# A fused attention and feed-forward kernel: inverse row sums of the first four jobs multiplied onto the result instead of onto the exponentials, and the low bits of all second-weight parts prepared on ScalarE

## The chip, the cores and the metric

The kernel runs on one core of one Trainium2 chip. The metric is device time in microseconds (us) of one execution. Three executions of the kernel before gave 1086.21, 1086.63 and 1086.92 us; the median is 1086.63.

## What is computed

Causal attention for 8 batches, 8 heads, 576 positions and a head width of 64, with a bias made of running sums of `s`, and after it a feed-forward layer with a piecewise quadratic activation:

```python
scores = scale * q @ k.T + min(bias, 0)            # bias[t, u] = -(cum[t] - cum[u]), cum = cumsum(max(s, 0))
attn = exp(where(causal, -1e9, scores) - rowmax)
attn = attn / (sum(attn, -1) + 1e-9)
x = (attn @ v)                                     # reordered to 4608 rows of 512
h = x @ w_in                                       # 512 -> 2048
g = where(h >= 1, h, where(h <= -1, 0, (h + 1) ** 2 / 4))
out = g @ w_out                                    # 2048 -> 512
```

The two weight matrices arrive as 64-bit numbers, 8 bytes an element.

## The kernel before

**Jobs.** The attention is cut into 64 jobs: for each batch, first the four head pairs with query rows 0 to 319 (tiles of 64, 128 and 128 rows), then the four pairs with rows 320 to 575 (two tiles of 128). A head of a tile goes through `scores`: TensorE makes the scores in PSUM (L439 in the first twelve jobs, L442 and L443 later), VectorE adds the mask, takes the row minimum and writes SBUF (L448), ScalarE turns it into exponentials with their row sums (L459).

**The first four jobs** (batch 0, first half) are "plain": all in 32-bit floats. When both heads of a tile have their exponentials, `plain_t` makes the inverse row sums `rs` on VectorE (L473, L474) and multiplies them onto the exponentials in place: GpSimd does the first head (L479), ScalarE the second (L477). Then TensorE transposes the scaled blocks into a PSUM bank `pp` (L482; two banks of the tag "h" take turns), and ScalarE copies them to `pt` (L483). One job later `att_out` multiplies `pt` with `v` (L531) into a bank `px` of the "y" tags. The four `px` stay in their banks until the scale of the first weights is known; then `x_split` makes two 16-bit parts of each for the feed-forward, on ScalarE (L559) and VectorE (L560). All later jobs go another way (`weights_t`, 16-bit parts, transposed by DMA).

**Weights.** Each matrix comes in 16 parts of 128 x 512 elements, called `wir` for the first and `wor` for the second. `decode` rebuilds a part: ScalarE takes the high word (L208), VectorE shifts it (L209), takes its peak (L211), and ORs in low bits (L223). These low bits are prepared before, either on ScalarE (L219, 8-bit source, bias and scale) or on VectorE (L222, a 16-bit shift by 13); the table `ACT_LOW` says which parts go to ScalarE: the even ones of both matrices. `split` then makes the two 16-bit parts that the matmuls use: L260 on ScalarE, and L268 on VectorE or L263, L265 and L266 on GpSimd and ScalarE. It needs a scale from the peaks of a group of parts. For the second matrix there are two groups of eight; for each, `scale` runs a small chain of VectorE and TensorE steps: a transpose of the peaks (`row_wo`), a maximum (`top_wo`), a broadcast by matmul (`col_wo`) through banks of the tags "y2" and "y3", and a reciprocal (`r_wo`, L237 and L238). The first matrix has one such chain for all of it (`row_wi`, `top_wi`, `t_wi` cast, `col_wi`, `t_wi` copy, `shares`); the first `x_split` waits for its end.

**The feed-forward.** For each half of a batch, 16 steps `ffn_h` (12 matmuls each, L601), an eviction on ScalarE and VectorE (`u` L613, L616, L617, then the parts of `g`, L627 on ScalarE and L628 on GpSimd), and 16 steps `ffn_y` (12 matmuls each, L640). The `u` tiles have four buffers of tag "u".

**Order.** The program text interleaves all this by slots: one part of the first weights every three attention slots, then the decode of the second weights beside the first feed-forward steps. A scheduler then orders each engine's queue; what an engine has in its queue runs in that order.

Of the kernel before, what the change touches and what calls it, by code (L numbers as in the profile page):

```python
# [9 lines left out]
F32 = mybir.dt.float32  # L10
# [4 lines left out]
AF = mybir.ActivationFunctionType  # L15
ALU = mybir.AluOpType
# [4 lines left out]
B, H, S, D = 8, 8, 576, 64  # L21
DM, DFF = 512, 2048
P = 128
# [7 lines left out]
QT = [(0, 64, 64)] + [(64 + P * i, P, 64 + P * (i + 1)) for i in range(4)]  # L31
HALF = [(0, 320, (0, 1, 2)), (320, 256, (3, 4))]
BIG = 1e9
EPS = 1e-9
# [18 lines left out]

Y_LAG = 2

ACT_LOW = {'wi': range(0, 16, 2), 'wo': range(0, 16, 2)}
POOL_LO = {'wi': (0, 2, 4, 6, 8, 10), 'wo': range(1, 16, 2)}
POOL_SCALE = ('wi',)

# [17 lines left out]
def attention_ffn(ctx: ExitStack, tc: tile.TileContext, qT, kT, vn, s, w_in, w_out, yT):  # L77
    nc = tc.nc
    LOADQ, CUMQ, FIRSTQ = nc.sync, nc.scalar, nc.sync
    V, A, G, T = nc.vector, nc.scalar, nc.gpsimd, nc.tensor  # L80

    cp = ctx.enter_context(tc.tile_pool(name="cp", bufs=1))
    ap = ctx.enter_context(tc.tile_pool(name="ap", bufs=2))
    gp = ctx.enter_context(tc.tile_pool(name="gp", bufs=2))
    dp = ctx.enter_context(tc.tile_pool(name="dp", bufs=1, space=DRAM))
    ps_s = ctx.enter_context(tc.tile_pool(name="ps_s", bufs=2, space=PSUM))
    ps_h = ctx.enter_context(tc.tile_pool(name="ps_h", bufs=2, space=PSUM))
# [10 lines left out]
    ident = cp.tile([P, P], F32, name="ident")  # L98
# [78 lines left out]
    class Weights:  # L177
        def __init__(self, name, src, held, out, tag, groups, by_rows=False):
# [8 lines left out]
            self.raw = {}  # L187
            self.act_low, self.pool_lo = ACT_LOW[name], POOL_LO[name]

# [151 lines left out]
    X = {}  # L341

    NP = B * NPAIR
    raws, pts_, vts, pbs, sums = {}, {}, {}, {}, {}

    def whole(n, hf):
        return jobs.index((n, hf)) < F32_JOBS

    def plain(n, hf):
        return jobs.index((n, hf)) < PLAIN_JOBS  # L350

    def operands(n, hf):
        return whole_tiles[jobs.index((n, hf)) % 2]
# [70 lines left out]
    def scores(n, i, hd, c0, c1):  # L424

        off, R, W = QT[i]
        qo = off - HALF[i // 3][0]
        if hd == 0 and c0 == 0:
            sums[n, i] = ap.tile([P, 2], F32, tag="sm", bufs=4, name=f"sm{n}_{i}")
            pbs[n, i] = []  # L430
        if c0 == 0:
            Pt = ap.tile([P, SP], F32, tag="p", bufs=4, name=f"p{n}_{i}_{hd}")
            pbs[n, i].append(Pt)
            G.memset(Pt[:R, W:W + D], 0.0)
        Pt = pbs[n, i][hd]
        sc = ps_s.tile([P, 512], F32, tag="s", name=f"s{n}_{i}_{hd}_{c0}")
        if whole(n, i // 3):
            Q, K = operands(n, i // 3)
            T.matmul(sc[:R, :c1 - c0], Q[:KC, hd, qo:qo + R], K[:KC, hd, c0:c1], start=True, stop=True)  # L439
        else:  # L440
            (Q1, K1), (Q2, K2) = split_tiles
            T.matmul(sc[:R, :c1 - c0], Q1[:, hd, qo:qo + R], K1[:, hd, c0:c1], start=True, stop=False)  # L442
            T.matmul(sc[:R, :c1 - c0], Q2[:KC, hd, qo:qo + R], K2[:KC, hd, c0:c1], start=False, stop=True)  # L443
        mn = mins.pop((n, i, hd), None)
        m2 = ap.tile([P, 1], F32, tag="mn", bufs=6, name=f"mn{n}_{i}_{hd}_{c0}")
        mo = 448 - off + c0
        with tc.high_priority(offset=TTR_LEAD):
            ttr[0] = V.tensor_tensor_reduce(  # L448
                out=Pt[:R, c0:c1], in0=sc[:R, :c1 - c0], in1=mask[:R, mo:mo + c1 - c0],
                scale=-0.125, scalar=3.0e38 if mn is None else mn[:R],  # L450
                op0=ALU.add, op1=ALU.min, accum_out=m2[:R],
            ).ins
        if late:
            with tc.issue_after(ttr[0]):
                late.pop(0)()
        if c1 < W:
            mins[n, i, hd] = m2
            return
        A.activation(  # L459
            Pt[:R, :W], Pt[:R, :W], AF.Exp, bias=m2[:R], scale=-1.0, accum_out=sums[n, i][:R, hd:hd + 1]  # L460
        )
        if hd:
            weights_t(n, i)

    def plain_t(n, i):

        off, R, W = QT[i]
        h_off, N, tiles = HALF[i // 3]
        if i == tiles[0]:
            pts_[n, i // 3] = ap.tile([P, 2 * (tiles[-1] + 1), N], F32, tag="pt", bufs=2, name=f"pt{n}_{i // 3}")  # L470
        PT = pts_[n, i // 3]
        rs = ap.tile([P, 2], F32, tag="rs", bufs=4, name=f"rs{n}_{i}")
        V.tensor_scalar(rs[:R], sums.pop((n, i))[:R], EPS, 2.0 ** -12, ALU.add, ALU.mult)  # L473
        V.reciprocal(rs[:R], rs[:R])  # L474
        for hd, Pt in enumerate(pbs.pop((n, i))):
            if hd:
                A.activation(Pt[:R, :W], Pt[:R, :W], AF.Copy, scale=rs[:R, 1:])  # L477
            else:
                G.tensor_scalar(Pt[:R, :W], Pt[:R, :W], rs[:R, :1], 1.0, ALU.mult, ALU.mult)  # L479
            pp = ps_h.tile([P, 512], F32, tag="h", name=f"pp{n}_{i}_{hd}")  # L480
            for j in range(i + 1):
                T.transpose(pp[:, j * R:(j + 1) * R], Pt[:R, j * P:(j + 1) * P], ident[:R, :R])  # L482
            A.copy(  # L483
                PT[:, hd:2 * (i + 1):2, off - h_off:off - h_off + R],
                pp[:, :(i + 1) * R].rearrange("p (j r) -> p j r", r=R),
            )

    def weights_t(n, i):

        off, R, W = QT[i]  # L490
        hf = 0 if i < 3 else 1
        h_off, N, tiles = HALF[hf]
        if plain(n, hf):
            plain_t(n, i)
            return
        if i == tiles[0]:
            pts_[n, hf] = ap.tile([P, 4 * (tiles[-1] + 1), N], F16, tag="pt", bufs=2, name=f"pt{n}_{hf}")
        PT = pts_[n, hf]
        PB = ap.tile([P, i + 1, 4, P], F16, tag=f"pb{hf}", name=f"pb{n}_{i}")
        rs = ap.tile([P, 2], F32, tag="rs", bufs=4, name=f"rs{n}_{i}")  # L500
        V.tensor_scalar(rs[:R], sums.pop((n, i))[:R], EPS, 2.0 ** -12, ALU.add, ALU.mult)
        V.reciprocal(rs[:R], rs[:R])  # L502
        tiles2 = pbs.pop((n, i))
        pv, pw = (Pt[:R, :W + D].rearrange("p (j c) -> p j c", c=P) for Pt in tiles2)
        his, los = ([PB[:R, :, 2 * hd + l, :] for hd in range(2)] for l in range(2))
        G.tensor_scalar(his[0], pv, rs[:R, :1], 1.0, ALU.mult, ALU.mult)  # L506
        A.activation(tiles2[1][:R, :W], tiles2[1][:R, :W], AF.Copy, scale=rs[:R, 1:])  # L507
        G.tensor_scalar(his[1], pw, 1.0, 1.0, ALU.mult, ALU.mult)  # L508
        G.tensor_tensor(los[1], pw, his[1], ALU.subtract)  # L509

        def rest():
            V.scalar_tensor_tensor(los[0], pv, rs[:R, :1], his[0], ALU.mult, ALU.subtract)  # L512
            nc.sync.dma_start_transpose(
                out=PT[:, :4 * (i + 1), off - h_off:off - h_off + R],
                in_=PB[:R].rearrange("p j g c -> p (j g c)"),
            )

        late.append(rest)

    def att_out(n, hf):  # L520

        b, p = n // NPAIR, n % NPAIR
        h_off, N, tiles = HALF[hf]
        nj = tiles[-1] + 1
        PT = pts_.pop((n, hf))
        if plain(n, hf):
            px = ps_y.tile([P, 512], F32, tag=f"y{p}", name=f"px{n}_{hf}")
            for j in range(nj):
                lo = max(0, j * P - h_off)
                for hd in range(2):  # L530
                    T.matmul(  # L531
                        px[hd * D:(hd + 1) * D, lo:N], vraw[b, p][:, j, hd * D:(hd + 1) * D],
                        PT[:, 2 * j + hd, lo:], start=(j == 0), stop=(j == nj - 1),
                    )
            held[n, hf] = px
            return
        px = ps_s.tile([P, 512], F32, tag="s", name=f"px{n}_{hf}")
        steps = [(j, vl, pl) for j in range(nj) for vl, pl in ((0, 0), (1, 0), (0, 1))]
        for m, (j, vl, pl) in enumerate(steps):
            lo = max(0, j * P - h_off)  # L540
            for hd in range(2):
                T.matmul(  # L542
                    px[hd * D:(hd + 1) * D, lo:N],
                    vts[n][:, vl, j, hd * D:(hd + 1) * D],
                    PT[:, 4 * j + 2 * hd + pl, lo:],
                    start=(m == 0), stop=(m == len(steps) - 1),
                )
        x_split(n, hf, px, w1.shares)

    held = {}  # L550
# [162 lines left out]
    with tc.high_priority(offset=SCALE_LEAD):  # L713
# [4 lines left out]
        for c in range(NW - NKT, NW):  # L718
            w1.split(c)
    att_out(*jobs[NPAIR - 1])  # L720
    for n, hf in jobs[:NPAIR]:
        x_split(n, hf, held.pop((n, hf)), shares0)
# [61 lines left out]
```

## Time and profile before

| | |
|---|---|
| median of three runs | 1086.63 us |
| the profiled execution | 1084.4 us |
| its span | 1082.6 us |
| granted TensorE clock over the span | 0.992 |
| busy: TensorE, VectorE, ScalarE, GpSimd | 1010.8, 851.4, 722.7, 665.9 us |

The span begins with the first instruction and ends with the last; 1.8 us of the execution lie around it. Times in the rows count from the span's start. PE is TensorE, DVE VectorE, ACT ScalarE, POOL GpSimd, SP the queue that issues most transfers. The first weights are decoded from about 6 to 69 us, the plain jobs run from 14 to 92 us, the first `ffn_h` matmul starts at 94 us, and the second weights are decoded from 35 to 131 us.

### The profile page before, as it was taken

The numbers are of one execution on the slowest core, as the hardware profiler recorded it, in microseconds if no ns is written. First come the engines' busy times: TensorE is split into PE (matmuls) and PEld (weight loads), VectorE is DVE, ScalarE is ACT, GpSimd is POOL, SyncE is SP. The second block draws the span as 40 slices with busy tenths as digits, with TensorE's granted clock in tenths as the row PEclk, the third lists the DMA queues.
The fourth block names the chain that finished last, engine by engine and source line by source line (L and its number), as shares of the span: only waits on it lengthen the run. The fifth ranks groups of instructions, "written<-read, shape, count | busy, mean of one in ns | idle before, by whom it ended". The sixth has DMA issues, their size and how long they took to land.

```text
span 1082.6 us, 24990 instructions
## 1 busy us (share of the span) xinstructions
PE 1010.8 (93%) x8494; PEld 775.7 (72%) x8494; DVE 851.4 (79%) x2370; ACT 722.7 (67%) x1707; POOL 665.9 (62%) x1139
## 2 busy tenths in 40 slices
PE   2657799999999999999999999999999999999998
PEld 1334466787778777887778777787778777887787
DVE  6898975688788888887788787788788787887533
ACT  4886774667577755877577765777577755877433
POOL 3764775675567656665577656665567656665422
PEclk9999899999999999999999999999999999999999
DMA  8974444455376873777366553765376662666300
GB/s 257 226 210 143 102 96 102 89 134 143 78 169 146 137 139 83 171 140 141 91 164 142 141 132 93 162 135 143 80 171 142 135 142 68 158 127 137 70 25 20
DMA packets 300839, 140.33 MB, mean 130 GB/s; under 512 B 237608, under 2 KB 286632, under 8 KB 300712
## 3 DMA queue, kind: packets, MB, share of 16 engines
q1 hardware_dynamic: 291008, 128.80, 53.1%
q10 hardware_dynamic: 9704, 9.93, 3.0%
q8 instruction: 67, 1.10, 0.4%
q14 instruction: 60, 0.49, 0.1%
HBM read 71.00 MB, written 9.73 MB: 75 GB/s over the span
## 4 chain that ended last, share of the span: by engine, by line
PE 66%; DVE 14%; ACT 7%; DMA 5%; issue 4%; POOL 2%; ACTq 1%; SPq 1%; DVEq 0%; POOLq 0%
PE h L601 27%; PE y L640 27%; PE px L542 4%; PE s L442 3%; PE s L443 3%; DVE pb L512 2%; DVE p L448 2%; PE s L439 2%; DVE h L616 2%; ACT u L613 1%; ACT p L459 1%; DVE K2s L398 1%; DMA v<-in_v_dram 1%; DMA wir<-in_moe_w_in_dram 1%; ACT o L654 1%
## 5 line engine op out<-in xcount | busy, mean ns | idle before, releaser
L601 PE MATMUL h<-x,WI 128*128 128x256 f16 (+1 forms) x3072 | 456.9, 289 | 4.0 <-ACT x L559 2.7
L640 PE MATMUL y<-g,WO 128*128 128x256 f16 (+1 forms) x3072 | 447.6, 287 | 4.0 <-DVE WO L268 2.6
L601 PEld LDWEIGHTS <-WI 128*128 128x128 f16 x3072 | 286.8, 99 | 94.4 <-issue 12.7
L640 PEld LDWEIGHTS <-WO 128*128 128x128 f16 x3072 | 286.8, 98 | 87.4 <-issue 5.0
L628 POOL TENSOR_TENSOR g<-u,g 128x320 f16<-128x320 f32 (+1 forms) x256 | 206.8, 808 | 162.1 <-ACT g L627 154.2
L459 ACT ACTIVATE p<-p,mn 64x64 f32<-64x64 f32 (+4 forms) x320 | 179.6, 561 | 107.2 <-DVE mn L448 82.3
L613 ACT ACTIVATE u<-h,ub,us 128x320 f32<-128x320 f32 (+1 forms) x256 | 149.5, 585 | 130.9 <-PE h L601 126.7
L616 DVE SCALAR_TENSOR_TENSOR h<-h,ws,u 128x320 f32<-128x320 f32 (+1 forms) x256 | 132.8, 519 | 89.1 <-ACT u L613 85.6
L506 POOL TENSOR_SCALAR pb<-p,rs 128x256 f16<-128x256 f32 (+4 forms) x148 | 93.4, 631 | 138.3 <-DVE rs L502 85.7
L509 POOL TENSOR_TENSOR pb<-p,pb 128x256 f16<-128x256 f32 (+4 forms) x148 | 156.6, 1058 | 9.8
L448 DVE CUSTOM_DVE_ANT_0 p<-s,mask 64x64 f32<-64x64 f32 (+4 forms) x320 | 135.0, 422 | 31.4 <-PE s L443 20.4
L512 DVE SCALAR_TENSOR_TENSOR pb<-p,rs,pb 128x256 f16<-128x256 f32 (+4 forms) x148 | 127.1, 859 | 21.3 <-POOL pb L506 20.8
L617 DVE SCALAR_TENSOR_TENSOR u<-u,r,h 128x320 f32<-128x320 f32 (+1 forms) x256 | 130.5, 510 | 7.3
L442 PE MATMUL s<-K1s,Q1s 128*128 128x288 f32 (+4 forms) x312 | 118.1, 379 | 9.8 <-DVE Q1s L397 4.1
L507 ACT ACTIVATE p<-p,rs 128x192 f32<-128x192 f32 (+4 forms) x148 | 84.3, 569 | 49.6 <-DVE rs L502 47.1
L627 ACT CAST g<-u 128x320 f16<-128x320 f32 (+1 forms) x256 | 108.2, 423 | 11.0 <-DVE u L617 10.8
L508 POOL TENSOR_SCALAR pb<-p 128x256 f16<-128x256 f32 (+4 forms) x148 | 89.1, 602 | 19.6 <-ACT p L507 14.6
L443 PE MATMUL s<-K2s,Q2s 68*128 68x288 f32 (+4 forms) x312 | 96.1, 308 | 0.0
L542 PEld LDWEIGHTS <-vt 128*64 128x64 f16 x1464 | 67.3, 111 | 19.7 <-issue 14.6
L542 PE MATMUL px<-pt,vt 128*64 128x256 f16 (+3 forms) x1464 | 77.9, 254 | 1.3 <-DMA pt<-pb 1.0
L442 PEld LDWEIGHTS s<-K1s,Q1s 128*128 128x128 f32 (+1 forms) x312 | 56.6, 181 | 19.1 <-PE s L443 4.0
L398 DVE TENSOR_TENSOR K2s<-rk,K1s 64x1152 fp32r<-64x1152 f32 (+1 forms) x52 | 63.2, 1216 | 5.9 <-ACT K1s L395 4.7
(130 smaller groups left out, 1035.0 us busy)
## 6 DMA issues: line engine op xcount, KB each, us to landing
rk<-in_k_dram SPq DMA_DIRECT2D x56, 288.0 KB
wir<-in_moe_w_in_dram SPq DMA_DIRECT2D x16, 512.0 KB
v<-in_v_dram SPq DMA_DIRECT2D x32, 256.0 KB
wor<-in_moe_w_out_dram SPq DMA_DIRECT2D x16, 512.0 KB
rk<-in_k_dram SPq DMA_DIRECT2D x48, 160.0 KB
rq<-in_q_dram SPq DMA_DIRECT2D x48, 160.0 KB
rq<-in_q_dram SPq DMA_DIRECT2D x56, 128.0 KB
out_dram<-o ACTq DMA_DIRECT2D x32, 160.0 KB
```

The lines of the kernel that those rows point to most:

```text
L442: T.matmul(sc[:R, :c1 - c0], Q1[:, hd, qo:qo + R], K1[:, hd, c0:c1], start=True, stop=False)
L448: ttr[0] = V.tensor_tensor_reduce(out=Pt[:R, c0:c1], in0=sc[:R, :c1 - c0], in1=mask[:R, mo:mo + c1 - c0], scale=-0.125, scalar=3.0e38 if m ...
L459: A.activation(Pt[:R, :W], Pt[:R, :W], AF.Exp, bias=m2[:R], scale=-1.0, accum_out=sums[n, i][:R, hd:hd + 1])
L509: G.tensor_tensor(los[1], pw, his[1], ALU.subtract)
L512: V.scalar_tensor_tensor(los[0], pv, rs[:R, :1], his[0], ALU.mult, ALU.subtract)
L542: T.matmul(px[hd * D:(hd + 1) * D, lo:N], vts[n][:, vl, j, hd * D:(hd + 1) * D], PT[:, 4 * j + 2 * hd + pl, lo:], start=(m == 0), stop=(m ...
L601: T.matmul(h[:, :N], WI[4 * kt + ft // 4][:, wl, ft % 4 * P:(ft % 4 + 1) * P], x[:, kt, xl], start=(n == 0), stop=(n == 3 * NKT - 1),)
L613: first = A.activation(u, h[:, :N], AF.Relu, bias=ubi[b], scale=usc[b]).ins
L616: V.scalar_tensor_tensor(h[:, :N], h[:, :N], wsc[b], u, ALU.mult, ALU.max)
L617: V.scalar_tensor_tensor(u, u, r, h[:, :N], ALU.min, ALU.mult)
L628: G.tensor_tensor(g[:, 1], u, g[:, 0], ALU.subtract)
L640: T.matmul(ys[b, hf, m][:, :N], WO[8 * (m // 2) + ft // 2][:, wl, c0:c0 + P], g[:, gl], start=(ft == 0 and n == 0), stop=(ft == NFT - 1 an ...
```

## The change

1. `ACT_LOW` for the second weights holds all 16 parts: the low bits of the eight odd ones are prepared by L219 on ScalarE instead of L222 on VectorE.
2. In the plain jobs the exponentials are transposed as they are, head by head, right after L459. The eight-line loop with the multiplications on GpSimd and ScalarE is gone. The inverse row sums are still made on VectorE, in tiles of an own tag with six buffers.
3. `att_out` of a plain job turns the inverse row sums into a row: six matmuls with a broadcast of `rp` as weights and the identity as moving data fill a bank `rx` of tag "h" (64 equal rows for each head). ScalarE copies `rx` to `z` in SBUF (tag "u"), VectorE multiplies it with `px` into `z`. `x_split` reads `z`; the `px` banks are free earlier.

```diff
-ACT_LOW = {'wi': range(0, 16, 2), 'wo': range(0, 16, 2)}
+ACT_LOW = {'wi': range(0, 16, 2), 'wo': range(16)}
...
-        if hd:
+        if plain(n, i // 3):
+            plain_t(n, i, hd)
+        elif hd:
             weights_t(n, i)
...
-    def plain_t(n, i):
+    def plain_t(n, i, hd):
...
-        for hd, Pt in enumerate(pbs.pop((n, i))):
-            if hd:
-                A.activation(Pt[:R, :W], Pt[:R, :W], AF.Copy, scale=rs[:R, 1:])
-            else:
-                G.tensor_scalar(Pt[:R, :W], Pt[:R, :W], rs[:R, :1], 1.0, ALU.mult, ALU.mult)
...
+        if hd:
+            del pbs[n, i]
+            rs = rss[n, i] = ap.tile([P, 2], F32, tag="rp", bufs=6, name=f"rp{n}_{i}")
+            V.tensor_scalar(rs[:R], sums.pop((n, i))[:R], EPS, 2.0 ** -12, ALU.add, ALU.mult)
+            V.reciprocal(rs[:R], rs[:R])
...
-            held[n, hf] = px
+            rx = ps_h.tile([P, 512], F32, tag="h", name=f"rx{n}_{hf}")
+            for i in tiles:
+                off, R, _ = QT[i]
+                rs = rss.pop((n, i))
+                for hd in range(2):
+                    T.matmul(
+                        rx[hd * D:(hd + 1) * D, off - h_off:off - h_off + R],
+                        rs[:R, hd:hd + 1].to_broadcast([R, D]), ident[:R, :R], start=True, stop=True,
+                    )
+            z = held[n, hf] = gp.tile([P, N], F32, tag="u", bufs=4, name=f"z{n}_{hf}")
+            A.copy(z, rx[:, :N])
+            V.tensor_tensor(z, px[:, :N], z, ALU.mult)
             return
```

**The queue of TensorE at the end of the plain jobs.** Names are `s`, `pp`, `px` with the job, the tile and the head behind them, and a running number last. Before, from the last scores of job 3 (`s3_2_1`) to the first scores of the next half (`s0_3_0`):

```order
L439 MATMUL s3_2_1_0_661<-K2w_92,Q2w_91 128x320
L110 MATMUL row_wi_753<-ident_77,t_wi_751 1x128
L482 MATMUL pp3_1_0_632<-ident_77,p3_1_0_614 128x128 x2
L482 MATMUL pp3_1_1_637<-ident_77,p3_1_1_621 128x128 x2
L120 LDWEIGHTS ones_82
L120 MATMUL col_wi_759<-t16_wi_757,ones_82 128x1
L439 MATMUL s0_3_0_0_926<-K1w_90,Q1w_89 128x448
```

With the change, the same queue from the product of job 3 to the same scores:

```order
L527 MATMUL px3_0_800<-pt3_0_585,v0_3_189 64x320
L110 MATMUL row_wi_759<-ident_77,t_wi_757 1x128
L527 MATMUL px3_0_800<-pt3_0_585,v0_3_189 64x320
L527 MATMUL px3_0_800<-pt3_0_585,v0_3_189 64x192 x2
L527 MATMUL px3_0_800<-pt3_0_585,v0_3_189 64x64 x2
L536 MATMUL rx3_0_807<-ident_77,rp3_0_608 64x64 x2
L536 MATMUL rx3_0_807<-ident_77,rp3_1_636 64x128 x2
L536 MATMUL rx3_0_807<-ident_77,rp3_2_674 64x128 x2
L120 LDWEIGHTS ones_82
L120 MATMUL col_wi_765<-t16_wi_763,ones_82 128x1
L439 MATMUL s0_3_0_0_942<-K1w_90,Q1w_89 128x448
```

The broadcast `col_wi` stood behind transposes of job 3 whose data GpSimd and ScalarE had to scale; now all transposes of job 3 stand ahead of these rows, and between `row_wi` and `col_wi` stand the product of job 3 and its six `rx` matmuls.

**The queue of VectorE at the scale of the second weights' first group.** `h0_0_0` and `u0_0_0` belong to the first feed-forward step. Before, behind the first two evictions (L616, L617):

```order
L209 TENSOR_SCALAR WO13_139<-WO13_139 128x512
L222 TENSOR_SCALAR wor11_1051<-wor11_1051 128x512
L237 RECIPROCAL r_wo0_156<-bound_wo0_154 128x1
L338 TENSOR_SCALAR ys0_0_897<-gb0_783,bound_wo0_154 128x1
L512 SCALAR_TENSOR_TENSOR pb0_4_1084<-p0_4_0_978,rs0_4_1085,pb0_4_1084 128x5x128
L502 RECIPROCAL rs1_3_1211<-rs1_3_1211 128x2
L211 ISA sums2_144,peak_wo_153<-WO13_139 128x256
```

With the change, ahead of the first eviction:

```order
L331 RECIPROCAL gb0_789<-r0_775 128x1
L237 RECIPROCAL r_wo0_156<-bound_wo0_154 128x1
L223 SCALAR_TENSOR_TENSOR WO10_136<-wor8_838,WO10_136 128x512
L211 ISA sums2_144,peak_wo_153<-WO11_137 128x256
L211 ISA peak_wo_153 128x1
L327 TENSOR_SCALAR ws0_785<-us0_783 128x1
L332 TENSOR_SCALAR gb0_789<-gb0_789 128x1
L238 TENSOR_SCALAR r_wo0_156<-r_wo0_156 128x1
```

The reciprocal `r_wo0`, on which the first parts of `WO` for `ffn_y` wait, moved from behind the first two evictions to ahead of them.

More of the change, by code (lines that the diff above doesn't have):

```diff
@@ L343, in attention_ffn @@
     NP = B * NPAIR
-    raws, pts_, vts, pbs, sums = {}, {}, {}, {}, {}
+    raws, pts_, vts, pbs, sums, rss = {}, {}, {}, {}, {}, {}
     def whole(n, hf):
@@ L461, in scores @@
         )
-        if hd:
+        if plain(n, i // 3):
+            plain_t(n, i, hd)
+        elif hd:
             weights_t(n, i)
-    def plain_t(n, i):
+    def plain_t(n, i, hd):
         off, R, W = QT[i]
         h_off, N, tiles = HALF[i // 3]
-        if i == tiles[0]:
+        if i == tiles[0] and hd == 0:
             pts_[n, i // 3] = ap.tile([P, 2 * (tiles[-1] + 1), N], F32, tag="pt", bufs=2, name=f"pt{n}_{i // 3}")
[L471 to L474, printed above, removed]
-        for hd, Pt in enumerate(pbs.pop((n, i))):
-            if hd:
-                A.activation(Pt[:R, :W], Pt[:R, :W], AF.Copy, scale=rs[:R, 1:])
-            else:
[L479 to L486, printed above, removed]
+        PT, Pt = pts_[n, i // 3], pbs[n, i][hd]
+        pp = ps_h.tile([P, 512], F32, tag="h", name=f"pp{n}_{i}_{hd}")
+        for j in range(i + 1):
+            T.transpose(pp[:, j * R:(j + 1) * R], Pt[:R, j * P:(j + 1) * P], ident[:R, :R])
+        A.copy(
+            PT[:, hd:2 * (i + 1):2, off - h_off:off - h_off + R],
+            pp[:, :(i + 1) * R].rearrange("p (j r) -> p j r", r=R),
+        )
[4 more added lines that the diff above has]
+            V.reciprocal(rs[:R], rs[:R])
     def weights_t(n, i):
@@ L492, in weights_t @@
         h_off, N, tiles = HALF[hf]
-        if plain(n, hf):
-            plain_t(n, i)
-            return
         if i == tiles[0]:
@@ L534, in att_out @@
                     )
-            held[n, hf] = px
+            rx = ps_h.tile([P, 512], F32, tag="h", name=f"rx{n}_{hf}")
[6 more added lines that the diff above has]
+                        rs[:R, hd:hd + 1].to_broadcast([R, D]), ident[:R, :R], start=True, stop=True,
+                    )
+            z = held[n, hf] = gp.tile([P, N], F32, tag="u", bufs=4, name=f"z{n}_{hf}")
+            A.copy(z, rx[:, :N])
+            V.tensor_tensor(z, px[:, :N], z, ALU.mult)
             return
```

## The prediction

> **What bounds the kernel now.** I read the busy time of the engines in stretches first. Each row has start and end, length, then the busy time of PE, PEld, DVE, ACT and POOL, the granted clock, the DMA share and GB/s.
>
> ```profile
> 27.00:54.00 27.00, 18.38 (x55) 9.87 (x56) 23.72 (x72) 23.96 (x56) 21.44 (x28) 1.00 0.92 228
> 54.00:81.00 27.00, 16.20 (x51) 8.74 (x51) 26.38 (x83) 23.31 (x52) 17.65 (x23) 1.00 0.70 209
> 81.00:108.00 27.00, 20.40 (x80) 11.62 (x81) 23.27 (x88) 16.56 (x34) 12.24 (x17) 0.92 0.50 143
> 108.00:135.00 27.00, 20.42 (x126) 12.62 (x125) 27.00 (x59) 20.50 (x38) 19.20 (x21) 0.89 0.41 103
> 135.00:162.00 27.00, 27.00 (x201) 18.39 (x199) 21.16 (x54) 21.87 (x43) 21.96 (x30) 1.00 0.40 92
> 200.00:300.00 100.00, 100.00 (x868) 77.72 (x866) 78.49 (x216) 63.89 (x149) 62.70 (x104) 1.00 0.47 111
> ```
>
> There are two regimes. From 135 us on TensorE is busy without a gap (27.00 of 27, 100.00 of 100): whatever moves the start of that regime moves the end by as much, and an edit on another engine there is worth nothing. The change touches only work before it. From 27 to 135 TensorE idles 32.6 of 108 us and VectorE is the fullest engine: 23.72 + 26.38 + 23.27 + 27.00 = 100.4 of 108. So the question is how much earlier the work up to 135 us gets done.
>
> Second, the chain of waits from the start to 140 us (start, length, what):
>
> ```profile
> 54.72 4.70 DMA wir<-in_moe_w_in_dram
> ...
> 70.45 0.76 DVE wor L222
> ...
> 73.65 1.85 DVE wor L222
> ...
> 78.47 5.83 POOL p L479
> ...
> 101.08 4.32 DMA wor<-in_moe_w_out_dram
> ...
> 106.55 0.66 DVE wor L222
> ...
> 114.06 1.33 DVE wor L222
> ```
>
> It goes mostly through VectorE's decode of the weights. Four of the eight L222 that the change takes away lie on it (4.6 us), one of the multiplications that it takes away (L479), and two waits for weight transfers that it doesn't touch. Third, who waited for whom, for PE from 84 to 108 and from 108 to 135 us and for DVE from 27 to 140 us (total, times, longest):
>
> ```profile
> PE pp L482 <- POOL p L479: 7.4, 1, 7.4
> ```
> ```profile
> PE y L640 <- DVE WO L268: 2.6, 1, 2.6
> ```
> ```profile
> DVE WO L223 <- ACT wir L219: 1.5, 3, 0.8
> ...
> DVE t_wi L121 <- PE col_wi L120: 1.6, 1, 1.6
> ```
>
> The multiplication on GpSimd held the transposes, and `col_wi` stood behind them in TensorE's queue. The reader should see that the 7.4 us of TensorE are only 1.6 us for VectorE: it decoded second weights meanwhile.
>
> **The change part by part.** The sum is made against the profiled execution (1084.4 us, span 1082.6); the median of the runs is 1086.63, 2.2 more, and I carry the difference over to it.
>
> *Low bits.* The rows of the two ways to prepare them (duration in ns: least, median, most), and the group's mean:
>
> ```profile
> L222 DVE TENSOR_SCALAR wor<-wor x8: 722/740/1928, 38.5 to 127.2; 128x512 uint16<-128x512 uint16 x8
> ```
> ```profile
> L222 DVE TENSOR_SCALAR wor<-wor 128x512 uint16<-128x512 uint16 x8 | 7.8, 979 | 0.0
> ```
> ```profile
> L219 ACT ACTIVATE wor<-wor,floor_bias 128x512 uint16<-128x512 uint8 x8 | 11.5, 1434 | 0.1
> ```
>
> VectorE loses eight L222: 8 x 0.74 = 5.9 us by the median, 7.8 by the mean, which holds the stretched ones. I take 5.9, since what stretches one instruction may stretch the next in its place. ScalarE gains 8 x 1.434 = 11.5 us.
>
> The Trainium skill speaks against this move: the page "ScalarE: Activation LUTs", section "Rules for kernel authors", says to use VectorE, not ScalarE, for simple arithmetic. The rows agree in price (1434 ns against 740); by that rule the eight cost 8 x 0.69 = 5.6 us, and the sum below, -4.8, would be +0.8 instead (1087.4). The first rival is this rule as a mechanism of this kernel.
>
> *Scaling.* What leaves, and the nearest rows of what comes:
>
> ```profile
> L479 POOL TENSOR_SCALAR p<-p,rs x12: 432/965/5816, 20.0 to 87.2; 64x64 f32<-64x64 f32 x4, 128x192 f32<-128x192 f32 x4, 128x320 f32<-128x320 f32 x4
> ```
> ```profile
> L477 ACT ACTIVATE p<-p,rs x12: 333/447/562, 20.0 to 87.2; 64x64 f32<-64x64 f32 x4, 128x192 f32<-128x192 f32 x4, 128x320 f32<-128x320 f32 x4
> ```
> ```profile
> L483 ACT COPY pt<-pp 128x384 f32<-128x384 f32 x8 | 3.7, 462 | 1.6 <-PE pp L482 1.6
> ```
> ```profile
> L616 DVE SCALAR_TENSOR_TENSOR h<-h,ws,u 128x320 f32<-128x320 f32 x15 | 8.3, 552 | 1.4 <-ACT u L613 1.4
> ```
> ```profile
> L482 PE MATMUL pp<-ident,p 128*128 128x128 f32 x40 | 11.8, 434 | 14.2 <-POOL p L479 13.0 <-ACT p L477 0.9 <-ACT pt L483 0.4
> ```
>
> - VectorE gets four products `z`, 128 x 320 with one operand in PSUM, as L616: 4 x 0.552 = 2.2 us. So VectorE nets -5.9 + 2.2 = **-3.7** (with the mean, -5.6). It is the fullest engine, so I count this whole. The reciprocals stay, as many as before, and nothing urgent waits for them any more.
> - The wait for `col_wi` goes: **-1.6**. Bounds: 0, if the six `rx3` matmuls and the product of job 3, now ahead of `col_wi`, are as late; -5.8, the whole L479 of the chain. I stay at the wait that VectorE itself shows, since next late is its own decode work, which stands between `top_wi` and `shares` in both orders.
> - Ready `r_wo` before the first evictions (the order of VectorE): the 2.6 us in which `ffn_y` waited for L268 can go. Next late is the cast of `g` on ScalarE (L627), so I take **-1.0** of 0 to -2.6.
> - ScalarE: +11.5, less L477 (12 x 0.447 = 5.4), plus four copies `z` (at most the 462 ns of a 384-wide one, 1.8): +7.9 us. Its idle time from 27 to 135 is 108 - 84.3 = 23.7 us, and that covers it on the whole. In order it doesn't quite: VectorE's L223 already waits 1.5 us for L219, and eight more L219 in a fuller queue, with 4 products waiting for a copy, I put at as much again: **+1.5**, of 0 to +7.9 (cover gone).
> - TensorE: 24 `rx` matmuls, at most 24 x 0.434 = 10.4 us. From 27 to 108 it idles 8.6 + 10.8 + 6.6 = 26.0 us: 0, and 10.4 if that cover were gone. No DMA is added or moved past a queue's end; later loads go out when L223 frees a buffer.
> - GpSimd: twelve L479 go. It isn't on the path but for the one counted: 0. `x_split` from SBUF instead of PSUM: the same operations, 0.
>
> The one L479 of 5.8 us, against a median of 965 ns, ran while VectorE had no gap. The Trainium skill's page "SBUF — State Buffer", section "SBUF: two separate sides", says that GpSimd and a VectorE instruction in a two-port mode shut each other out of a shared port for the length of an instruction. The trace agrees with that; the sum with the whole excess over the least (5.8 - 0.4 = 5.4) instead of 1.6 would be -8.6 (1078.0).
>
> Sum: -3.7 - 1.6 - 1.0 + 1.5 = -4.8 us. Profiled 1084.4 becomes 1079.6, the median 1086.63 becomes **1081.8**.
>
> **The rivals.**
>
> *ScalarE becomes the bound (slower).* Place: 108 to 135 us, where ScalarE idles 6.5 us. After the first `x_split` its queue will hold seven L219 of second weights instead of four, 3 x 1.434 = 4.3 us more, in front of the evictions L613 and L627. What it waits for, from 92 to 135 us:
>
> ```profile
> ACT WO L208 <- DMA wor<-in_moe_w_out_dram: 3.4, 3, 1.4
> ACT g L627 <- DVE u L617: 3.2, 2, 2.2
> ```
>
> It decides if more than 6.5 - 4.3 = 2.2 us of these waits stay. Then the 4.3 lie on the path, VectorE's saving is worth nothing there, and with the -1.6 of `col_wi` the result is +2.7: 1089.3. For it: the waits are 6.6 us. Against: part of them is on VectorE, which gets quicker. 15%.
>
> *Loads pace it anyway (no change).* The DMA share is 0.92 from 27 to 54 us, and two pieces of the chain, 4.70 and 4.32 us, are transfers that start when a buffer comes free and then take their time. If the loads set the pace, a freer VectorE only waits more, and -1.0 is left: 1085.6. Against: VectorE is at 27.00 of 27 when the DMA share is 0.41. 17%.
>
> *More than the sum (faster).* If the stretched durations go with the instructions (L222 by the mean, -5.6), the whole 2.6 us of `ffn_y` and half of the POOL piece of the chain (-2.9) are won, and ScalarE costs 0.5: -10.6, 1076.0. 13%.
>
> **How the numbers follow.** The forecast, faster by 2 to 8 us, has 55%. A measurement of this kernel can tell about 0.2% (2.2 us) from no change. Faster: 55 + 13 = 68%; same 17%; slower 15%. The range takes the forecast, the case of no change and half of the larger gain: from 1076.5 to 1087.5; the upper end also holds a ScalarE cost of up to 7.2 of the 7.9 us (-6.3 + 7.2 = +0.9), the lower end the two ends -5.6 and -2.6 with -1.6 and nothing for ScalarE (-9.8, 1076.8).
>
> **What would show it.** Right: the chain has no POOL piece at 78 to 84 us and no wait for `col_wi`; the first `x_split` (91.90 in this row) starts about 2 to 5 us earlier; VectorE's busy time to 135 us falls by about 4 us; the wait of `ffn_y` for L268 shrinks; then all of the 200 to 300 us pattern comes earlier by the same amount.
>
> ```profile
> 91.90 1.37 ACT L559 ACTIVATE x<-px,shares 128x320 f16<-128x320 f32 x3
> ```
>
> Wrong: VectorE waits for L219 by several us, or ScalarE stands at 26 of 27 us in a stretch and PE waits for `u`; or TensorE reaches its gapless regime no earlier than before although the first `x_split` is early.

## The result and the profile after

Four executions of each kernel, in turns on one chip: the changed kernel takes 1075.74 us (median; 1075.36 to 1077.5), the kernel before 1086.78 us (1086.21 to 1089.4). The ratio is 0.9903, with a 95% interval of 0.9876 to 0.9929, so 11 us faster (7.7 to 13.5), where 4.8 were forecast. The changed kernel measured twice more, in other comparisons, gave 0.9919 (0.9891 to 0.9948) and 0.9922 (0.9901 to 0.9943): 8.5 to 9 us. The direction was right; the size was about twice the forecast.

The profiled execution takes 1077.5 us, its span 1075.7. Its stretches, in the columns of the table of before (start and end, length, busy PE, PEld, DVE, ACT, POOL, granted clock, DMA share, GB/s):

```profile
27.00:54.00 27.00, 21.18 (x79) 13.13 (x79) 21.51 (x73) 23.78 (x56) 18.82 (x27) 0.86 0.97 246
54.00:81.00 27.00, 21.06 (x91) 12.57 (x91) 25.32 (x79) 24.53 (x51) 11.91 (x20) 0.51 0.62 193
81.00:108.00 27.00, 18.57 (x58) 9.21 (x57) 24.88 (x88) 20.18 (x36) 11.10 (x12) 0.68 0.53 141
108.00:135.00 27.00, 23.49 (x150) 15.90 (x149) 26.50 (x73) 24.03 (x44) 17.94 (x26) 0.88 0.59 128
```

From 27 to 135 us VectorE is busy for 98.2 us (100.4 before; about 4 less were forecast), ScalarE for 92.5 (84.3): ScalarE now stands at 24 of 27 in three of the four stretches. TensorE idles 23.7 us there instead of 32.6. Of the 8.9 us between, 5.9 are the new `rx` matmuls, which fill idle time:

```profile
L536 PE MATMUL rx<-ident,rp 128*64 128x128 f32 x32 | 4.0, 397 | 0.0
L536 PE MATMUL rx<-ident,rp 64*64 64x64 f32 x16 | 1.9, 329 | 2.7 <-ACT pt L477 2.6
```

The chain of waits can be followed back only to 114.65 us in this trace, so it tells nothing of the time before. Two further traces of the changed kernel (`e12_after_third` and `e18_after_look` below) follow it to the start. The GpSimd piece at 78 to 84 us is gone from both. The transfers of the second weights are not: they make up 13.6 and 12.7 us of the first 140, where the chain of before had one piece of 4.32. L219 of second weights, now on ScalarE, has eight pieces of 10.6 and 9.6 us together. From `e12_after_third`:

```profile
89.96 6.09 DMA wor<-in_moe_w_out_dram
...
97.83 1.40 ACT wor L219
...
99.98 7.47 DMA wor<-in_moe_w_out_dram
...
110.36 1.32 ACT wor L219
...
112.66 1.33 ACT wor L219
```

Summed by engine over their 195 longest pieces, ScalarE holds 39.4 and 31.8 us of these two chains (22.4 and 14.4 in two traces of before) and VectorE 40.3 and 34.2 (42.2 and 52.5). So in the changed kernel the way to the steady stage goes through ScalarE about as much as through VectorE. In the first trace, who waits for whom on PE from 84 to 108 us, and on DVE from 27 to 140 us (total, times, longest):

```profile
PE col_wi L120 <- DVE t_wi L118: 4.5, 1, 4.5
PE s L439 <- DVE mn L448: 2.3, 2, 1.4
PE h L608 <- DVE u L624: 1.5, 1, 1.5
```
```profile
DVE WO L209 <- ACT WO L208: 3.2, 2, 1.9
DVE WI L268 <- ACT WI L260: 2.3, 5, 0.6
DVE p L448 <- PE s L439: 1.8, 2, 1.5
DVE WO L223 <- ACT wor L219: 0.8, 1, 0.8
DVE WO L223 <- ACT wir L219: 0.7, 2, 0.4
```

VectorE no longer waits for `col_wi`, as forecast, and TensorE's 7.4 us behind L479 are gone; but at the same place TensorE now waits 4.5 us for VectorE's cast of `t_wi`. So the first `x_split` starts only 1.0 us earlier (90.94 against 91.90; 2 to 5 were forecast):

```profile
90.94 1.90 ACT L566 ACTIVATE x<-z,shares 128x320 f16<-128x320 f32 x4
```

The scale of the first second-weight group comes 10 us earlier, before (first row) and after:

```profile
110.84 0.14 DVE L238 TENSOR_SCALAR r_wo<-r_wo 128x1 f32<-128x1 f32 x1
```
```profile
100.52 0.14 DVE L238 TENSOR_SCALAR r_wo<-r_wo 128x1 f32<-128x1 f32 x1
```

A good mark for the whole of the early work is the first eviction `u` of the second batch, because shortly before it (from TensorE's sixth `ffn_h` of the second half on) both kernels have the same order of instructions on TensorE. In the traces of before and of after it starts at:

```profile
243.94 0.62 ACT L613 ACTIVATE u<-h,ub,us 128x320 f32<-128x320 f32 x1 [0.64 <-PE h L601]
```
```profile
238.11 0.62 ACT L620 ACTIVATE u<-h,ub,us 128x320 f32<-128x320 f32 x1 [0.63 <-PE h L608]
```

That is 5.8 us of the 6.9 between these two spans. With the further traces below (three of before and four of after in all) the means are 245.2 and 238.1, 7.1 us apart, of 9.2 us between the mean spans (1084.1 and 1074.9). The 2.1 us left arise behind it, where TensorE has the same order of instructions in both.

### The profile page after: what moved, and what is told of

Read it like the earlier page. It is cut to its first block, busy times and chain, and to the rows that moved or that the text cites. A ratio compares the mean times of both kernels' runs of the same rounds, so it can differ in the third digit from the quotient of the medians.

```text
span 1075.7 us, 25058 instructions
## 1 busy us (share of the span) xinstructions
PE 1013.7 (94%) x8542; PEld 780.5 (73%) x8542; DVE 847.0 (79%) x2366; ACT 728.9 (68%) x1707; POOL 650.8 (61%) x1127
## 4 chain that ended last, share of the span: by engine, by line
PE 65%; DVE 11%; ACT 4%; issue 4%; DMA 2%; POOL 2%; ACTq 1%; DVEq 0%; POOLq 0%
PE h L608 27%; PE y L647 26%; PE px L549 4%; PE s L442 3%; PE s L443 3%; DVE pb L508 2%; DMA pt<-pb 2%; DVE h L623 2%; DVE p L448 2%; ACT u L620 1%; PE s L439 1%; DVE K2s L398 1%; DVE Q1s L397 1%; DVE u L624 1%; ACT p L459 1%
## 5 line engine op out<-in xcount | busy, mean ns | idle before, releaser
L459 ACT ACTIVATE p<-p,mn 64x64 f32<-64x64 f32 (+4 forms) x320 | 179.6, 561 | 115.5 <-DVE mn L448 90.5
L549 PEld LDWEIGHTS <-vt 128*64 128x64 f16 x1464 | 67.5, 111 | 21.1 <-issue 16.9
L434 POOL MEMSET p<- 128x64 f32 (+1 forms) x320 | 44.9, 154 | 41.7 <-PE pp L476 18.8
```

Of the source, the lines that this page charges most:

```text
L459: A.activation(Pt[:R, :W], Pt[:R, :W], AF.Exp, bias=m2[:R], scale=-1.0, accum_out=sums[n, i][:R, hd:hd + 1])
L549: T.matmul(px[hd * D:(hd + 1) * D, lo:N], vts[n][:, vl, j, hd * D:(hd + 1) * D], PT[:, 4 * j + 2 * hd + pl, lo:], start=(m == 0), stop=(m ...
```

## The experiments

Every measurement is a ratio to the kernel before, taken on one chip in turns; I turn it into us with 1086.6. The kernel before measured against itself stands first, since it shows how far to trust a ratio.

**The unchanged kernels again** (no edit).

> The kernel before once more, unchanged. Theory 'early work' (the whole gain of the change, about 11 us between the medians, comes from work before 165 us): ratio 1.000, and its profile shows the first evictions u at the same times as the first profile (u number 16 at about 164 us) and the last at about 1075 us, within 1 us. Rival 'late stalls' (the profiled pair differs by only 3.7 us at 165 us and by 8.4 us at the last u; the rest is stalls of TensorE on transfers in the long even part, which come and go between executions or with the phase): ratio 1.000 as well, but this profile has other stalls between 165 and 1075 us than the first one, by 2 us or more in sum.

Measured: 0.9981 (0.9964 to 0.9997), medians 1084.42 and 1086.44. A kernel against itself can look 2 us faster, so I draw nothing from a difference of 2 us between two kernels alone.

> The changed kernel once more. Both theories: ratio 0.990 within 0.002 (about 1076 us). Early work: u number 16 starts about 8 to 11 us before that of the kernel before in a profile of this call. Late stalls: it starts 3 to 5 us before, as in the first pair, and the distance grows later in the run. The granted clock of TensorE between 54 and 81 us was 0.51 in the first profile of the changed kernel and 1.00 before: if that comes from the program, it is again under 0.7; if it is chance, it is not.

> The changed kernel unchanged, as the reference for the three others on the same chip. By its two earlier measurements 0.990 to 0.992 of the kernel before.

Measured: 0.9919 and 0.9922, medians 1077.43 and 1077.57. I take 0.992, 8.7 us, as the gain in what follows. The 16th `u`, on which the first two expectations turn, starts at 166.2 us in the trace of the kernel before and at 159.6 in that of the changed one: 6.6 us apart, between the two theories.

**Each part alone.** The first run is the kernel before with the new table, the second the changed kernel with the old table:

```diff
-ACT_LOW = {'wi': range(0, 16, 2), 'wo': range(0, 16, 2)}
+ACT_LOW = {'wi': range(0, 16, 2), 'wo': range(16)}
```

> Only the table of the low bits is changed (all second-weight parts on ScalarE), the scaling stays as before. If VectorE's work sets the early time: 8 x 0.74 = 5.9 us less on VectorE, little lost to ScalarE, 1081 to 1083. Rival 'ScalarE is the bound' (11.5 us more on it, nothing taken off): 1086 or slower. If the parts need each other (the low bits fill the ScalarE time that the scaling frees): near 1085.

> Only the scaling is changed, the low bits of the odd second-weight parts stay on VectorE. By the terms of the prediction (+2.2 products on VectorE, -1.6 wait for col_wi, -1.0 wait for WO): about 1086. Rival 'the transposes that waited on GpSimd and the freed banks carry the gain': -6 us or more, under 1081.

Measured: low bits alone 0.9942 (0.9924 to 0.9959), 6.3 us; scaling alone 0.9966 (0.9948 to 0.9984), 3.7 us (against the kernel before run again in the same comparison: 4.6 and 2.2). The parts add up to the whole, 10.0 or 6.8 against 8.8 or 7.0. So the low bits give their 4.4 us or somewhat more. The scaling gives more than the 0.4 us of its forecast, but how much more is not settled, since 2.2 us is no more than a kernel can show against itself.

The traces of the two runs tell where the gains lie. With the low bits alone the second batch's first `u` starts at 239.2 us (245.2 in the mean before) and the rest takes 839.2 us (837.9 to 840.2 before): all of the gain comes early. With the scaling alone, in an execution that is one of the quickest of its run (1080.0 us), it starts at 242.3 us and the rest takes 835.9: 2.9 us come early, and about as much comes behind that mark.

**Half of the low bits** (the kernel before; the odd parts of one group only):

```diff
-'wo': range(0, 16, 2)}
+'wo': (0, 1, 2, 3, 4, 5, 6, 7, 8, 10, 12, 14)}         # the second run: (0, 2, 4, 6, 8, 9, 10, ..., 15)
```

> The kernel before, with the low bits of second-weight parts 0 to 7 all on ScalarE (four of the eight L222 gone, those of parts 1, 3, 5, 7). Theory 'VectorE time' (each L222 counts its 0.74 us wherever it stands before 135 us): about half of what all eight gave, -2.3 us against the unchanged kernel run again. Theory 'scale of the first group' (what counts is how early r_wo of group 0 and the first x_split come): nearly all of the gain, -4 us, r_wo of group 0 ends near 105 us as with all eight.

> The kernel before, with the low bits of second-weight parts 8 to 15 all on ScalarE (the L222 of parts 9, 11, 13, 15 gone). Theory 'VectorE time': about half of what all eight gave, -2.3 us against the unchanged kernel run again. Theory 'scale of the first group': less than 1 us, since these four run after 108 us, and r_wo of group 0 stays at 110 us.

Measured: 0.9976 (0.9965 to 0.9988) and 0.9975 (0.9959 to 0.9991), 2.6 and 2.7 us. Each half gives about half, wherever it stands before 135 us, though both are little above the 2 us that a kernel can show against itself. So VectorE's time counts, and the first group's scale shows no special place.

**The earlier scale alone** (the kernel before, with the chain of the first group in other banks):

```diff
-top = column_max(t, f"{self.name}{g}", (ps_y, "y2"))
+top = column_max(t, f"{self.name}{g}", (ps_s, "s") if g == 0 else (ps_y, "y2"))
...
-spread(bound, top, f"{self.name}{g}", (ps_y, "y3"))
+spread(bound, top, f"{self.name}{g}", (ps_s, "s") if g == 0 else (ps_y, "y3"))
```

> The kernel before, with only the row maximum and the spread of the first second-weight scale (w2.scale of group 0) in the score banks instead of the two banks that the held products of jobs 2 and 3 occupy. The inverse scale r_wo of group 0 can then be made before the first x_split. Theory 'banks' (the scaling's gain comes from the held products leaving the banks earlier, so that r_wo, the splits of the first second weights and the first y matmuls come earlier): r_wo ends about 6 us earlier (105 instead of 110.8 us), the wait of the y matmul for the split part goes (2.6 us), and the time falls by 2 to 4 us against the kernel before. Theory 'multiplications' (the gain comes from the removed multiplications on GpSimd and the transposes that stood behind them): r_wo is earlier, but the time stays within 1 us of the unchanged kernel run again (ratio 0.998).

Measured: 1.002 (1.0005 to 1.0035). `r_wo` ends at 103.7 us, 7 us earlier, and the time doesn't fall. The term of 1.0 us for it falls.

**The multiplications of the exponentials.** Three edits of the kernel before, in `plain_t`; the first moves GpSimd's to ScalarE, the second leaves them out, the third leaves out ScalarE's too:

```diff
-            if hd:
-                A.activation(Pt[:R, :W], Pt[:R, :W], AF.Copy, scale=rs[:R, 1:])
-            else:
-                G.tensor_scalar(Pt[:R, :W], Pt[:R, :W], rs[:R, :1], 1.0, ALU.mult, ALU.mult)
+            A.activation(Pt[:R, :W], Pt[:R, :W], AF.Copy, scale=rs[:R, hd:hd + 1])
```

> The kernel before, with the twelve multiplications L479 of the exponentials moved from GpSimd to ScalarE, where their twelve sisters L477 already are. ScalarE gets 12 x 0.447 = 5.4 us more. Theory 'multiplications': the 5.83 us multiplication of the chain and the 7.4 us wait of TensorE for it go, shares0 comes 1.6 to 3 us earlier, the time falls by 1.5 to 3 us. Theory 'banks': the wait goes, but VectorE fills it with later decode work as before; the time changes by less than 1 us either way (ratio 0.997 to 0.999 like the unchanged kernel).

> The kernel before without the twelve multiplications L479 on GpSimd (the even heads of the first four jobs stay unscaled, so that part of the result is left out); nothing takes their place. The prediction priced their going at -1.6 us, with -1.0 for the earlier scale. Theory 'GpSimd costs' (moving them to ScalarE gave nothing since ScalarE paid as much, and spare ones cost 3.8 us in the changed kernel): -3.5 to -5 us. Rival 'waits only': -1 to -2.6 us.

> The kernel before without any of the 24 multiplications of the exponentials, L477 on ScalarE and L479 on GpSimd (the first four jobs stay unscaled, so that part of the result is left out); nothing takes their place. Theory 'ScalarE is nearly as full as VectorE' (its time costs 0.8 us per us, as the spare low bits showed): 5.4 us less on ScalarE give 4 us more than leaving out L479 alone. Rival 'ScalarE has cover' (the prediction's price, 1.5 us for 7.9): 1 us more. What lies between this run and the scaling done alone is the price of the 24 transposing multiplications on TensorE and the four copies and products z, which the prediction put at 2.2 us.

Measured: moved 1.0004 (0.999 to 1.0019); GpSimd's left out 1.0017 (1.0004 to 1.0029); both left out 0.9945 (0.9928 to 0.9961). To take the multiplications off GpSimd gains nothing; to take ScalarE's away as well gains 6.0 us against the kernel before, and 7.8 against the run without GpSimd's alone (4.7 to 11 by the ends of the intervals). TensorE's waits from 27 to 140 us show a part of why. Without GpSimd's:

```profile
PE s L439 <- DVE mn L448: 15.4, 11, 3.3
PE pp L480 <- ACT p L477: 7.7, 3, 3.6
PE col_wi L120 <- DVE t_wi L118: 2.8, 1, 2.8
```

and without both (`pp` is L478 there):

```profile
PE s L439 <- DVE mn L448: 11.1, 11, 2.8
PE col_wi L120 <- DVE t_wi L118: 4.7, 1, 4.7
...
PE pp L478 <- ACT pt L479: 2.1, 3, 0.8
```

The transposes no longer wait for GpSimd's L479 (13.1 us in that window before), but for the twin, ScalarE's L477, 7.7 us. It stands in ScalarE's queue between the weights' L208, L219 and L260. Only when both are gone does the wait go. Then the first `x_split` starts at 86.93 us (90.70 without GpSimd's alone, 91.90 before) and the second batch's first `u` at 236.91 (246.88 without GpSimd's alone).

Two things limit this. ScalarE's multiplications were not left out alone. And the run that moves GpSimd's to ScalarE has twelve multiplications more there, some 5 us, than the run that leaves them out; TensorE waits 11.0 us for ScalarE's multiplications, and yet the kernel is not slower (1.0004 against 1.0017). So a us of ScalarE at this place has no fixed price: what is shown is that both multiplications together cost 6 us, not that ScalarE's queue is the reason.

Between the run without both and the scaling alone (0.9945 and 0.9966) lie 2.3 us, for `rx`, the copies and the products `z`; the forecast had 2.2. The traces of the two runs split the difference (their spans are 2.9 us apart): the scaling alone is 5.4 us later at the second batch's first `u` (242.26 against 236.91) and 2.5 us quicker behind it (835.9 against 838.4). So the new operations cost nearer 5 us than 2 early on, as far as one trace of each tells, and the agreement with 2.2 is luck.

**Spare work in the changed kernel.** Each run adds operations of the sort that the change removed or added, into a buffer that nobody reads: eight shifts on VectorE, eight low-bit preparations on ScalarE, twelve multiplications on GpSimd.

```diff
+V.tensor_scalar(spare16, src, 13, None, ALU.logical_shift_right)                     # odd wor parts
...
+A.activation(spare16, src[:, :500], AF.Identity, bias=floor_bias, scale=2.0 ** -5)   # odd wor parts
...
+G.tensor_scalar(spare, Pt[:R, :W], 0.5, 1.0, ALU.mult, ALU.mult)                     # first heads
```

> The changed kernel with eight spare shifts on VectorE, made from the odd second-weight parts as L222 made them but written to a buffer that nobody reads; ScalarE keeps all low bits. This puts the VectorE time back without giving ScalarE less. Theory 'VectorE time': each counts its 0.74 us, +5.9 us against the changed kernel run again. Theory 'stretched': the mean of the kernel before, 0.98 us each, +7.8 us. Theory 'waits' (the low bits gained because the chain decode waits less, not because VectorE is full): less than +2 us.

> The changed kernel with eight spare low-bit preparations on ScalarE (1.43 us each, 11.5 us in all), made from the odd second-weight parts and written to a buffer that nobody reads. The prediction priced 7.9 us more on ScalarE at +1.5 us; at that rate +2.2 us against the changed kernel run again. Rival 'covered': ScalarE's idle time still hides it, within 1 us. Rival 'ScalarE is next': the reserve is used up, +5 us or more.

> The changed kernel with the twelve multiplications put back on GpSimd as spare work: of the same exponentials, at the same places, written to a buffer that nobody reads. Every other instruction stands where it did. Theory 'contention' (GpSimd's multiplications stretched VectorE's instructions, and the scaling gained because they went): VectorE's shifts L209 and sums L211 get longer by 2 to 4 us in all up to 135 us, and the time rises by 1.5 to 4 us against the changed kernel run again. Theory 'waits' (only that somebody waited for them counted): within 1 us.

Measured: 0.9992 (0.9976 to 1.0008), 1.0006 (0.9992 to 1.002) and 0.9955 (0.9937 to 0.9972); against the changed kernel of the same comparison (1077.57 us) the medians are 8.6, 9.4 and 3.8 us longer. The eight shifts (3.6 to 11.6 us by the ends of the intervals) cost 1.08 us each by the medians, more than the median of L222 (0.74) and about its mean (0.98), which I had not taken. ScalarE's 11.5 us (5.3 to 12.9 by the ends) cost 0.8 us for each us, four times the rate of the forecast, as the rival 'ScalarE is next' had it. TensorE's longest waits in that run, 27 to 140 us, are for VectorE's row minimum (6.2 us in the first trace of the changed kernel) and for ScalarE's copies (4.3 for `pp` and 2.6 for `rx` there):

```profile
PE s L443 <- DVE mn L452: 10.1, 7, 4.5
PE pp L480 <- ACT pt L481: 6.9, 4, 2.2
...
PE rx L540 <- ACT pt L481: 3.4, 2, 2.6
```

GpSimd's spare multiplications, which nobody waits for and which leave the order of all other instructions as it was, cost 3.8 us by the medians; the intervals touch, so the size is not settled. VectorE's shifts L209 in the traces of `e12_after_third` and of this run, without and with them:

```profile
L209 DVE TENSOR_SCALAR WO<-WO 128x512 int32<-128x512 int32 x27 | 12.4, 460 | 5.3 <-ACT WO L208 5.3
```
```profile
L211 DVE TENSOR_SCALAR WO<-WO 128x512 int32<-128x512 int32 x26 | 14.0, 541 | 3.9 <-ACT WO L210 3.9
```

They are 81 ns longer each. But the four traces of the changed kernel have 460 to 508 ns (the three of before 603 to 637), so only 33 ns lie beyond what traces of one kernel differ by. The other forms of VectorE show no such difference on balance, and up to 185 us this trace is only 1.1 us behind, so stretching is a part of the price at most.

**To hand GpSimd work of the full engines** (the changed kernel; could have beaten both):

```diff
-POOL_SCALE = ('wi',)
+POOL_SCALE = ('wi', 'wo')
...
-POOL_LO = {'wi': (0, 2, 4, 6, 8, 10), 'wo': range(1, 16, 2)}                         # the other run
+POOL_LO = {'wi': (0, 2, 4, 6, 8, 10, 12, 14), 'wo': range(1, 16, 2)}
```

> The changed kernel with the eight scalings of the odd second-weight parts ahead of their low parts (L265 for the second weights) moved from ScalarE to GpSimd. Theory 'ScalarE is next' (11.5 us more on ScalarE cost 9.3 us, so less on it gains): ScalarE loses eight 128x512 scalings, and the time falls by 2 to 4 us against the changed kernel. Rival 'contention' (GpSimd's work stretches VectorE's): the eight run on GpSimd beside a full VectorE, and the time is the same or up to 4 us longer. This one could beat both kernels.

> The changed kernel with the low parts of first-weight parts 12 and 14 made on GpSimd instead of VectorE: VectorE loses two L268 (0.97 us each), GpSimd gets two scalings and two subtractions. Theory 'VectorE time' at the price that eight spare shifts showed (8.6 us for 5.9): -2 to -3 us. Rival 'late GpSimd': the parts come late, since these splits stand right ahead of the first evictions, and the time rises by 1 us or more.

Measured: 0.9962 (0.9945 to 0.9978) and 0.996 (0.9944 to 0.9976), both about 4 us slower than the changed kernel at 0.992. What VectorE or ScalarE is spared doesn't pay for what GpSimd takes on; whether through later weight parts or through stretched VectorE work, these two runs don't tell. The changed kernel stays the fastest of all that compute the whole.

**A look more at each** (no edit, one execution each).

> The kernel before once more, for its trace alone. Theory 'shown in every trace' (the later half of the gain belongs to the change): TensorE's clock dips at 190 to 200 us, and from the eviction u number 32 to the end it takes 837.9 to 838.7 us, as in both earlier traces. Rival 'chance': one or both of these are missing.

> The changed kernel once more, for its trace alone. Theory 'shown in every trace': no clock dip at 180 to 200 us (one of its three traces has one), and from the eviction u number 32 to the end 836.1 to 837.0 us. Rival 'chance': a dip, or 838 us or more.

Measured: 1088.01 and 1076.06 us. In the kernel before, the second batch's first `u` starts at 246.00 and the rest takes 840.2 us; TensorE's clock dips again. In the changed kernel: 237.78, 836.5 us, and a dip. So 'shown in every trace' holds for the length of the rest in its order (before 837.9 to 840.2, after 836.2 to 837.6), not for its bounds nor for the dip, which is in three of three traces of before and in two of four of after. Most of the rest's difference lies between the `u` evictions 143 and 159 (counted from 0): 61.5, 60.2 and 60.1 us before, 58.4, 58.9, 58.5 and 58.5 after. There SP's queue issues a load of `v` between two transposes; before and after (the call is the third row of each):

```profile
688.71 0.39 SPq L290 DMA_DIRECT2D v<-in_v_dram  x1
689.49 1.84 SPq L513 DMA_TRANSPOSE pt<-pb  x1
691.38 1.66 SPq L291 DMA_DIRECT2D v<-in_v_dram  x1
```
```profile
682.97 0.40 SPq L290 DMA_DIRECT2D v<-in_v_dram  x1
683.74 1.95 SPq L509 DMA_TRANSPOSE pt<-pb  x1
685.75 0.58 SPq L291 DMA_DIRECT2D v<-in_v_dram  x1
```

The issue takes 1.66 us instead of 0.58, in all three traces of before (1.66, 2.02, 1.77); the transpose behind it comes later, and TensorE waits 1.0 to 1.3 us for `pt`. Of the traces of all kernels here, nine of the ten with the new scaling pass this stretch in under 59 us, and all ten without it take 59.6 or more. So these 2 us go with the program. The slow issue is not the whole of it: with the earlier scale alone it takes 0.81 us at this place and the stretch 60.8, with first-weight parts on GpSimd 0.58 and 59.9. Why an issue at that place is slow in the one and not in the other wasn't tried and stays open.

## Why the prediction was wrong

Point by point:

- **VectorE is the fullest engine, and its time counts whole.** Right: half of the low bits gave about half, and eight spare shifts cost 8.6 us. The term -5.9 + 1.5 = -4.4 for the low bits measured -4.6 to -6.3. That it came so near is partly luck. By the spare shifts the eight L222 are worth 8.6 us, not 5.9; what the low bits gave leaves 2.3 to 4.0 us as the price of 11.5 us on ScalarE (an estimate from these runs). Both sizes were too small, and they stand against each other.
- **`rx` and `z`.** The rows were right: 5.9 us of TensorE fill idle time, and `z` costs 0.47 us a product. The whole was not: all the new operations cost nearer 5 us than 2.2 up to the second batch.
- **The wait for `col_wi`, -1.6, and the earlier `r_wo`, -1.0.** Both waits went, and neither was worth anything alone: with GpSimd's multiplications left out VectorE's wait for `col_wi` is gone and the first `x_split` starts 1.2 us earlier, and the time does not fall; nor does it with the scale 7 us earlier. That VectorE's own work is next late was right for `col_wi`, where TensorE now waits 4.5 us for the cast of `t_wi`. For the transposes it was not: there L477 on ScalarE was next late.
- **The multiplications and ScalarE, +1.5. This is the step that failed**: "Its idle time from 27 to 135 is 108 - 84.3 = 23.7 us, and that covers it on the whole." The sum gave the twelve L479 nothing but the 1.6 us of one wait, and it set the twelve L477 that leave against the eight L219 that come, as if ScalarE's time were the same anywhere. Leaving out L479 gave nothing, and leaving out L477 as well gave 6.0 us (at the second batch's first `u` 8.3: 245.2 in the mean before, 236.9). The scaling with its new operations gave 2.9 us up to there, where the prediction had 0.4. Nine of the twelve L477 stood from 27 to 81 us, between the exponentials and the transposes, where the quoted rows had ScalarE at 23.96 and 23.31 of 27; the idle time was in other stretches, above all from 81 to 135 us (10.4 and 6.5 of 27). That this is the reason is likely and not shown, since twelve more of them on ScalarE did not make the kernel slower.
- **From 135 us on, an earlier start moves the end by as much. Here a term was missing**: 7.1 us at the second batch's first `u` became 9.2 at the end, and these 2.1 us are about half of what the forecast lacked. The stretch without gaps was not of one length; it has small stalls, and one of 2 us was in one program only. The sum had no term for that, and the cause of that stall stays open.

Of the rivals, 'ScalarE becomes the bound' did not come as a slower kernel, although its own condition was met: of the two waits quoted for it 3.0 us stay from 92 to 135 us (more than 2.2 were to decide), and ScalarE is busy 24.03 of 27 us from 108 to 135, in `e12_after_third` even 25.85. The price that it put on this was wrong, but it named the next bound rightly, as ScalarE's spare work (+9.4 us) and the L219 in the new chain show. The Trainium skill's rule in "ScalarE: Activation LUTs", section "Rules for kernel authors" (VectorE for simple arithmetic), would have made the low bits a loss (the prediction's +0.8 adds its 5.6 us to a sum that still holds the -4.4; in their place it would be +5.2); the runs have them gain 4.6 to 6.3 us, although L219 still takes 1433 ns, so for a move away from the fullest engine the measurement decides against it. 'Loads pace it anyway' did not come: the DMA share is 0.97 from 27 to 54 us (0.92 before), and the time fell all the same, though loads now hold 13 us of the chain. 'More than the sum' had the right time, 1076.0, and of its parts the stretched VectorE time fits the price of the spare shifts, while the GpSimd piece and the earlier `r_wo` were worth nothing alone; so its nearness is in part luck. For the same reason the larger sum with the whole excess of L479, 1078.0, is near the result without its cause being shown: the excess went when GpSimd's multiplications were left out, and the time did not fall. The Trainium skill's "SBUF — State Buffer", section "SBUF: two separate sides", is hardly borne out or refuted here: with the spare multiplications on GpSimd, VectorE's shifts are 33 to 81 ns longer than in the four traces without.

That the order of each queue changes with every edit limits all this: the run without GpSimd's multiplications does less work than the kernel before and was not faster. The prices are those of whole schedules.

## What to carry to other kernels

Before idle time is called a cover, look at it stretch by stretch and in the queue where the moved instruction stands: of the 23.7 idle us here, 16.9 were in the two later stretches, and nine of the twelve instructions in the two earlier ones. When a stall is to go because one of two parallel steps goes, ask what its twin waits for; leaving out GpSimd's changed nothing, leaving out both gave 6 us. Compare the parts at a mark inside the run as well as at its end: what looked like 2.3 us against a forecast of 2.2 was a loss of 5.4 early and a gain of 2.5 later in the traces. And give a steady stage a term for its own stalls where two traces of one kernel differ in it by a us or two.

## What the runs showed of the hardware

- TensorE's granted clock in the early stages is not one number for a program: the changed kernel shows 0.51 from 54 to 81 us in its first trace and 1.00 in its second, and the first `x_split` behind it starts at the same time (90.94 and 90.93 us). TensorE idles 5.9 and 7.0 of these 27 us. The row of the second trace:

```profile
54.00:81.00 27.00, 20.01 (x91) 11.94 (x92) 25.42 (x79) 24.69 (x51) 12.87 (x21) 1.00 0.62 193
```

- A dip to 0.83 or 0.84 over 10 us between 180 and 200 us appears in some traces. In the changed kernel the stretch between the `u` evictions 15 and 31 takes 75.6 and 75.5 us with it and 74.0 twice without. But eviction 31 (counted from 0) starts at 234.5 to 235.3 us in all four, so a price of the dip is not shown. TensorE has a gap there with and without it: it is busy 8.89 of the 10 us from 180 to 190 in all four.
- On VectorE, one form (L209) lasts 460 to 637 ns in the mean of a trace over the kernels of this case, and 460 to 508 over the traces of one kernel. Eight spare shifts of a median of 0.74 us cost 8.6 us, so here the median of a trace was below the price.
